# A fused Nyström attention and gated FFN kernel: Newton's S as 32 moving columns, and B's block forms made from PSUM

## Chip, cores, metric

One core of a Trainium2 chip. The metric is the device time of one execution in microseconds (us), taken by the device; medians and ranges are given over repeated executions. Slow runs of the kernel before are left out of its medians. Ratios are the mean time of one kernel's fast runs over the mean of the other's fast runs of the same rounds, so they are not quite the ratio of the medians that stand beside them. The intervals are 95% intervals.

## The reference, cut to what matters

```python
def _attn_ref(q, k, v):                      # q, k, v: 8 x 8 x 576 x 64
    m = 32
    q_lm = q.reshape(B, H, m, S // m, D).mean(axis=3)
    k_lm = k.reshape(B, H, m, S // m, D).mean(axis=3)
    A, Bm, C = sm(q, k_lm), sm(q_lm, k_lm), sm(q_lm, k)      # softmaxes
    Z = Bm^T / (|Bm|_1 * |Bm|_inf + 1e-06)
    for _ in range(6):
        Z = 2 * Z - Z @ Bm @ Z               # Newton's iteration, 32 x 32 for each head
    return A @ Z @ C @ v
# then, over the 4608 tokens: sigmoid(x @ w_gate) * (x @ w_val) @ w_out
```

The eight batches are woven together: while the tensor engine (PE) does the FFN of one batch, it also does the small attention matrices of the next.

The other engines bear their names of the profile: DVE is the vector engine, ACT the scalar engine, POOL is GpSimd, SP the SyncE, which issues DMAs, and PEld stands for the PE's weight loads. SBUF and PSUM are the two memories that the kernel puts its tiles in; it hands PSUM out in eight banks (BANKS = 8). Names of tiles that come up below: bs, sl and sa are the scores of B, C and A; cv is C·v; rtp turns the inverse row sums of A (rhl); an is A itself, made with them. `up` multiplies the rest of the attention (WT) into w_gate and w_val, which gives U and V; gp and vp are A times U and V, th the sigmoid's part of gp, ht the gated product, op the product with w_out, and ob its copy on the way out. s_5k and s_5q are the landmark sums of batch 5's k and q, from which GpSimd makes klm and bq.

## The kernel before

Four heads stand on the 128 partitions and two such groups lie side by side, so one 32 x 32 matrix for each of the eight heads is a tile of 128 x 2 x 32. To multiply it on the PE in one go it is spread into a **block form** of 128 x 128, with zeros off the blocks (`blk` is the mask of zeros and ones). Newton's iteration is kept as S = Z·B together with Y = Z·(C v): each step is S ← 2S − S·S and Y ← 2Y − S·Y. S is symmetric, so it serves as the fixed operand as it is.

```python
        # mid(b): B, its transpose, the square that Newton starts from
        E = sb.tile([128, 2, m], FP32, ...)
        act.activation(out=E, in_=bs, func=AF.Exp, scale=scale2)     # bs: PSUM
        ...                                                          # rs, rr: row sums on DVE
            act.mul(out=Bc[:, g, :], in_=E[:, g, :], mul=rr[:, g:g + 1])       # late batches
        dve.transpose(out=Bt..., in_=Bc...)
        spread(bdT, Bt)                                              # dve.tensor_mul with blk
        ...
            mm(out=s0[g], lhsT=bdT[:, g], rhs=bdT[:, g], ...)        # 128 columns
        s_at = [each(b, g).mul(sy[:, g, 0:128], s0[g], rc[:, g:g + 1]) ...]
        spread(bd, Bc)

        # newton(b), six iterations
                lo = 0 if it < ITERS - 1 else 128
                yield need(sy, banks=1)
                pn = bank([128, 2, 128 + D - lo], FP32, ...)
                for g in range(2):
                    mm(out=pn[:, g, :], lhsT=sy[:, g, 0:128], rhs=sy[:, g, lo:128 + D], ...)
                if lo == 0:
                    nsy = sb.tile([128, 2, 128 + D], BF16, ...)
                    dve.scalar_tensor_tensor(
                        out=nsy, in0=sy, scalar=2.0, in1=pn, op0=ALU.mult, op1=ALU.subtract)

        # front(b): the two halves of the landmark sums change places through DMA
                for c in range(2):
                    nc.sync.dma_start(out=other[what][64 * c:64 * c + 64], in_=s4[64 - 64 * c:128 - 64 * c])
```

The order of instructions is fixed when the kernel is built. A small model of the engines (the **recorder** below) is kept while the program is written down: it holds for every tile when it will have landed and for every engine when it will be free, and each time the PE has room it picks the next piece of work among those whose inputs have landed by then. `yield need(bd)` means "not before bd has landed".

The softmax here doesn't subtract the row's maximum and nothing guards it: scores larger than these inputs give would overflow.

## Time and profile before

| | before |
|---|---|
| median, range | 271.59 us, 271.58 to 271.88 (3 runs) |
| span of the profiled execution | 269.7 us |
| PE busy | 260.1 us, 96% |
| DVE busy | 193.3 us, 72% |

**Content** is the streaming time of all PE work in the built order (columns at 2.4 to the ns, but no less than 25 ns, plus 2 ns, plus 95 ns for each turn into or out of packed 32-column work; in the trace of before, matmuls of 512, 192, 96 and 32 columns start 216, 82, 42 and 25 ns behind their like, medians, and the 68 turns of the prediction have medians of 96 ns in and 95 out). **Waiting** is how much the start of a matmul in the trace falls behind the content ahead of it; I give how much it grows from 50 us on, where the kernel has its steady form. Before has 252.2 us of content and 4.0 us of waiting. These 4.0 are in part a residue of how I price the work: in the trace of e6 below, which has the same order and lacks no matmul, about 2 us of them stand at packed groups and the matmuls behind them, the rest in small pieces elsewhere. So only differences of waiting between kernels mean something.

### The profile page before, as it was taken

To read this page: it belongs to the slowest core of one execution; us is meant where nothing else is said; L and a number is where in the kernel's file an instruction comes from. 1 tells how busy PE (TensorE), PEld (TensorE's weight loads), DVE (VectorE), ACT (ScalarE), POOL (GpSimd) and SP (SyncE) were. 2 spreads that over 40 slices of the span, in tenths; PEclk is the share of its full clock that TensorE was granted. 3 is DMA by queue.
4 is the path that set the end of the run, shared out by engine and by line. 5 is a ranking of instruction groups with operands and counts; after the bars stand their busy time and mean duration, and the time that the engine had idled before them with its cause. 6 is when DMAs were issued, how large, how long until landed. Compare 5 with 4: busy or idle time off the path is not lost.

```text
span 269.7 us, 8019 instructions
## 1 busy us (share of the span) xinstructions
PE 260.1 (96%) x3089; PEld 167.0 (62%) x3123; DVE 193.3 (72%) x551; ACT 159.4 (59%) x413; POOL 96.2 (36%) x107
## 2 busy tenths in 40 slices
PE   8999999999999999999999999999999999999994
PEld 5877777757664666556646665556636664665443
DVE  4566888976899788948986778848968786963111
ACT  3663876866647754876477655875368643964001
POOL 8523231960874039511953078212922000000000
PEclk9999999999999999999999999999999999999999
DMA  6999999999795998889794989589530413101433
GB/s 94 193 206 205 205 206 206 205 203 172 141 194 115 204 170 121 181 135 199 141 221 72 182 157 203 129 139 199 124 90 12 97 41 80 41 0 41 117 103 92
DMA packets 62645, 38.00 MB, mean 141 GB/s; under 512 B 33552, under 2 KB 58128, under 8 KB 62608
## 3 DMA queue, kind: packets, MB, share of 16 engines
q0 software_dynamic: 23600, 18.88, 47.0%
q1 hardware_dynamic: 38896, 18.52, 31.4%
q8 instruction: 24, 0.39, 0.6%
q14 instruction: 13, 0.11, 0.1%
q10 hardware_dynamic: 112, 0.10, 0.1%
HBM read 37.75 MB, written 9.44 MB: 175 GB/s over the span
## 4 chain that ended last, share of the span: by engine, by line
PE 93%; ACT 2%; issue 2%; POOL 1%; DVE 0%; POOLq 0%; ACTq 0%
PE op L247 34%; PE gp L247 18%; PE vp L247 18%; PE idle_ps L247 3%; PE pn L247 2%; PE cv L247 2%; PE rb L247 2%; PE sc L247 1%; PE sa L247 1%; PE tp_q L252 1%; PE up_1g L247 1%; PE up_0g L247 1%; PE up_2g L247 1%; PE tp_k L252 1%; PE up_1v L247 1%
## 5 line engine op out<-in xcount | busy, mean ns | idle before, releaser
L247 PE MATMUL op<-wo_sb,ht 128*128 128x512 bf16 (+1 forms) x410 | 109.4, 373 | 2.1 <-issue 1.1
L153 ACT ACTIVATE th<-gp 128x288 bf16<-128x288 f32 x192 | 76.7, 415 | 48.4 <-PE gp L247 36.7
L153 DVE SCALAR_TENSOR_TENSOR ht<-th,vp 128x288 bf16<-128x288 bf16 x192 | 82.0, 448 | 21.9 <-ACT th L153 17.2
L247 PE MATMUL gp<-an,U 128*128 128x288 bf16 x384 | 78.5, 286 | 0.3
L247 PE MATMUL vp<-an,V 128*128 128x288 bf16 x384 | 78.4, 286 | 0.0
L247 PEld LDWEIGHTS <-ht 128*128 128x128 bf16 x444 | 39.9, 98 | 26.7 <-issue 5.8
L247 PEld LDWEIGHTS <-U 128*128 128x128 bf16 x384 | 35.9, 98 | 27.3 <-issue 2.5
L247 PEld LDWEIGHTS <-V 128*128 128x128 bf16 x384 | 37.5, 98 | 9.7 <-issue 0.2
L153 ACT ACTIVATE ob<-op 128x512 f32<-128x512 f32 (+1 forms) x31 | 18.2, 587 | 29.6 <-PE op L247 24.2
L153 DVE SCALAR_TENSOR_TENSOR sy<-sy,pn 128x384 bf16<-128x384 bf16 x35 | 19.2, 548 | 2.3 <-PE pn L247 1.9
L153 DVE TENSOR_SCALAR ob<-op 128x512 f32<-128x512 f32 (+2 forms) x7 | 4.2, 596 | 17.3 <-PE op L247 17.3
L247 PE MATMUL idle_ps<-idle_w 128*128 128x256 bf16 x86 | 14.8, 308 | 1.2 <-DVE idle_w L297 1.2
L247 PE MATMUL pn<-sy 128*128 128x192 bf16 (+1 forms) x84 | 13.1, 237 | 0.4 <-ACT kT L153 0.3
L153 DVE TENSOR_TENSOR an<-aexp,rb 128x384 bf16<-128x384 bf16 (+1 forms) x32 | 12.4, 446 | 0.3 <-PE rb L247 0.3
L247 PEld LDWEIGHTS <-sy 128*128 128x128 bf16 x88 | 8.1, 97 | 6.2 <-DVE sy L153 2.8
L153 ACT ACTIVATE aexp<-sa 128x288 bf16<-128x288 f32 x32 | 10.7, 418 | 1.5 <-PE sa L247 1.1
L247 PEld LDWEIGHTS <-idle_w 128*128 128x128 bf16 x86 | 8.5, 109 | 3.3 <-DVE idle_w L297 1.2
L247 PEld LDWEIGHTS <-WT 64*32 64x32 bf16 x384 | 3.8, 89 | 9.1 <-issue 6.6
L270 POOL DMA_DIRECT2D kn<-in_k_dram x9 | 7.0, 779 | 4.6 <-DMA wg_sb<-in_moe_w_gate_dram 2.1
L153 DVE CAST U<-up_0g 128x512 bf16<-128x512 f32 x8 | 5.5, 690 | 4.1 <-PE up_0g L247 4.1
L270 POOL DMA_DIRECT2D vn<-in_v_dram x8 | 6.3, 789 | 5.3 <-PE gp L247 4.5
L270 POOL DMA_DIRECT2D qn<-in_q_dram x9 | 6.8, 753 | 4.0 <-PE sm L247 2.2
(201 smaller groups left out, 349.7 us busy)
## 6 DMA issues: line engine op xcount, KB each, us to landing
vn<-in_v_dram POOLq DMA_DIRECT2D x8, 576.0 KB, 9.4
kn<-in_k_dram POOLq DMA_DIRECT2D x7, 576.0 KB, 8.1
qn<-in_q_dram POOLq DMA_DIRECT2D x7, 576.0 KB, 10.6
out_dram<-ob SPq DMA_DIRECT2D x53, 64.0 KB, 3.0
out_dram<-ob SPq DMA_DIRECT2D x17, 192.0 KB, 2.3
out_dram<-ob SPq DMA_DIRECT2D x18, 128.0 KB, 2.4
wg_sb<-in_moe_w_gate_dram POOLq DMA_DIRECT2D x3, 512.0 KB, 19.7
wv_sb<-in_moe_w_val_dram POOLq DMA_DIRECT2D x3, 512.0 KB, 21.0
```

Of the source, the lines that this page charges most:

```text
L153: f(**kw)
L247: nc.tensor.matmul(**kw)
L252: nc.tensor.transpose(**kw)
L270: nc.gpsimd.dma_start(out=t[:, hs], in_=src[b, hs].rearrange("h (p c) d -> p h (c d)", p=P6))
```

## The change

Its intent: in batches 2 to 7 the S part of the moving operand needs only 32 columns, because the product of a block form with a 32-column S is again a 32-column S. So `pn` shrinks from 192 to 96 columns. Since the fixed operand must still be the block form, the DVE has to make one (`sd`) in every step. Separately, B's block form `bd` is made straight from the exponentials in PSUM, B's transpose is made on the PE (`Bp`), and `bdT` is made from PSUM.

```diff
-        E = sb.tile([128, 2, m], FP32, name=f"E_{b}", tag="E")
+        late = b >= LATE
+        E = bs if late else sb.tile([128, 2, m], FP32, name=f"E_{b}", tag="E")
...
+        if late:
+            for g in range(2):
+                dve.scalar_tensor_tensor(
+                    out=bd[:, g], in0=E[:, g, None, :].to_broadcast([128, NP, m]),
+                    scalar=rr[:, g:g + 1], in1=blk, op0=ALU.mult, op1=ALU.mult)
+            yield need(bd, banks=1)
+            Bt = bank([128, 2, m], FP32, f"Bp_{b}")
+            for g in range(2):
+                mm(out=Bt[:, g], lhsT=bd[:, g], rhs=four, start=(g == 0), stop=(g == 1))
+        else:
+            (the DVE transpose, as before)
+        if b >= COMPACT:                                   # COMPACT = 2
+            Bs = sb.tile([128, 2, m], BF16, name=f"Bt_{b}", tag="Bt")
+            act.copy(out=Bs, in_=Bt)
...
-            mm(out=s0[g], lhsT=bdT[:, g], rhs=bdT[:, g], ...)
+            mm(out=s0[g], lhsT=bdT[:, g], rhs=Bs[:, g] if b >= COMPACT else bdT[:, g], ...)
...
-                    mm(out=pn[:, g, :], lhsT=sy[:, g, 0:128], rhs=sy[:, g, lo:128 + D],
+                    mm(out=pn[:, g, :], lhsT=sd[:, g], rhs=sy[:, g, lo:w + D],      # w = 32
...
+                    if compact:
+                        new = p[:, 2 * (w + D):].rearrange("p (g x) -> p g x", g=2)   # PSUM
+                        dve.scalar_tensor_tensor(
+                            out=new, in0=sy[:, :, 0:m], scalar=2.0, in1=pn[:, :, 0:m],
+                            op0=ALU.mult, op1=ALU.subtract)
                     nsy = ...                              # as before, 192 elements in place of 384
+                    if compact:
+                        sd = sb.tile([128, 2, NP, m], BF16, ...)
+                        dve.tensor_mul(
+                            out=sd, in0=blk[:, None].to_broadcast([128, 2, NP, m]),
+                            in1=new[:, :, None, :].to_broadcast([128, 2, NP, m]))
```

(cut: the constants, batch 0 and 1, the first `sd`, the norm's small tile moved to PSUM)

More of the change, by code (lines that the diff above doesn't have):

```diff
@@ L217 @@
     SWAP = 3
+    COMPACT = 2
     consts = ctx.enter_context(tc.tile_pool(name="consts", bufs=1))
@@ L350 @@
     model.free["dve"], model.free["act"] = 5.4, 6.6
+    four = consts.tile([128, m], BF16, name="four")
+    nc.vector.tensor_reduce(
+        out=four, in_=ident.rearrange("p (i l) -> p l i", i=NP), axis=AX.X, op=ALU.max)
     front_of, sums_of, lm_of, value_of, mid_of, norm_of, an_of, uv_of, step_at = ({} for _ in range(9))
-    square_of, turned_c, q_of = {}, {}, {}
+    square_of, turned_c, q_of, sd_of = {}, {}, {}, {}
     def copy(out, in_):
@@ L610, in mid @@
                 act.mul(out=Bc[:, g, :], in_=E[:, g, :], mul=rr[:, g:g + 1])
-        Bt = sb.tile([128, 2, m], BF16, name=f"Bt_{b}", tag="Bt")
-        dve.transpose(out=Bt.rearrange("p g l -> p (g l)"), in_=Bc.rearrange("p g l -> p (g l)"))
         bdT = sb.tile([128, 2, NP, m], BF16, name=f"bdT_{b}", tag="bdT")
         bd = sb.tile([128, 2, NP, m], BF16, name=f"bd_{b}", tag="bd", bufs=3)
+        if late:
[8 more added lines that the diff above has]
+        else:
+            Bt = sb.tile([128, 2, m], BF16, name=f"Bt_{b}", tag="Bt")
+            dve.transpose(out=Bt.rearrange("p g l -> p (g l)"), in_=Bc.rearrange("p g l -> p (g l)"))
+        if b >= COMPACT:
+            Bs = sb.tile([128, 2, m], BF16, name=f"Bt_{b}", tag="Bt")
+            act.copy(out=Bs, in_=Bt)
         def spread(dst, src):
+            if late:
+                return dve.tensor_mul(
+                    out=dst, in0=blk[:, None].to_broadcast([128, 2, NP, m]),
+                    in1=src[:, :, None, :].to_broadcast([128, 2, NP, m]))
             for g in range(2):
@@ L627, in mid @@
         yield need(model.landed[Bc.name] + (0.25 if b else 0.0), banks=1)
-        n1 = bank([128, 2, m], FP32, f"n1_{b}")
+        n1_cc = bank([128, 2 * m + 2], FP32, f"n1_{b}")
+        n1 = n1_cc[:, 0:2 * m].rearrange("p (g l) -> p g l", g=2)
         mm(out=n1, lhsT=blk, rhs=Bc, start=True, stop=(b > 0))
@@ L631, in mid @@
             mm(out=n1, lhsT=eps, rhs=idle_w[:, 0:2 * m], start=False, stop=True)
-        ce = sb.tile([128, 2], FP32, name=f"cc_{b}", tag="cc")
+        ce = n1_cc[:, 2 * m:] if b > 0 else sb.tile([128, 2], FP32, name=f"cc_{b}", tag="cc")
         dve.tensor_reduce(out=ce, in_=n1, axis=AX.X, op=ALU.max)
@@ L638, in mid @@
         dve.reciprocal(out=rc, in_=ce)
-        apart = 2 if b == 0 else 1
+        apart, w = 2 if b == 0 else 1, m if b >= COMPACT else 128
         yield need(bdT, banks=apart)
-        s0 = [bank([128, 2 // apart, 128], FP32, f"s0_{b}{x}") for x in range(apart)]
+        s0 = [bank([128, 2 // apart, w], FP32, f"s0_{b}{x}") for x in range(apart)]
         s0 = [s0[g % apart][:, g // apart] for g in range(2)]
         for g in range(2):
-            mm(out=s0[g], lhsT=bdT[:, g], rhs=bdT[:, g], start=(g == 0 or b == 0), stop=(g == 1 or b == 0))
-        sy = sb.tile([128, 2, 128 + D], BF16, name=f"sy_{b}_0", tag="sy0", bufs=2)
+            mm(out=s0[g], lhsT=bdT[:, g], rhs=Bs[:, g] if b >= COMPACT else bdT[:, g],
+               start=(g == 0 or b == 0), stop=(g == 1 or b == 0))
+        sy = sb.tile([128, 2, w + D], BF16, name=f"sy_{b}_0", tag="sy0", bufs=2)
         if b == 0:
             model.by_part.add(sy.name)
-        s_at = [each(b, g).mul(sy[:, g, 0:128], s0[g], rc[:, g:g + 1]) for g in range(2)]
+        s_at = [each(b, g).mul(sy[:, g, 0:w], s0[g], rc[:, g:g + 1]) for g in range(2)]
         if b == 0:
             square_of[b] = [(sy, s_at)]
-        spread(bd, Bc)
+        elif b >= COMPACT:
+            sd_of[b] = sb.tile([128, 2, NP, m], BF16, name=f"sd_{b}_0", tag="sd", bufs=2)
+            for g in range(2):
+                dve.scalar_tensor_tensor(
+                    out=sd_of[b][:, g], in0=s0[g][:, None, :].to_broadcast([128, NP, m]),
+                    scalar=rc[:, g:g + 1], in1=blk, op0=ALU.mult, op1=ALU.mult)
+        if not late:
+            spread(bd, Bc)
         aexp = sb.tile([128, 2, S], BF16, name=f"aexp_{b}", tag="aexp", bufs=2)
@@ L667, in scale_y @@
                 dve.tensor_mul(out=ysc, in0=rcs, in1=rc)
-                y_at = [each(b, g).mul(sy[:, g, 128:128 + D], cv[g], ysc[:, g:g + 1])
+                y_at = [each(b, g).mul(sy[:, g, w:w + D], cv[g], ysc[:, g:g + 1])
                         for g in range(2)]
@@ L671, in scale_y @@
                 y_at = [dve.tensor_scalar(
-                    out=sy[:, g, 128:128 + D], in0=cv[g], scalar1=rcs[:, g:g + 1],
+                    out=sy[:, g, w:w + D], in0=cv[g], scalar1=rcs[:, g:g + 1],
                     scalar2=rc[:, g:g + 1], op0=ALU.mult, op1=ALU.mult) for g in range(2)]
@@ L802, in newton @@
             sy, bd, _ = mid_of[b]
+            compact = b >= COMPACT
+            w = m if compact else 128
+            sd = sd_of.pop(b) if compact else sy[:, :, 0:128]
             y6 = sb.tile([128, 2, 2, D], BF16, name=f"y6_{b}", tag="y6")
             for it in range(ITERS):
-                lo = 0 if it < ITERS - 1 else 128
-                yield need(sy, banks=1)
-                pn = bank([128, 2, 128 + D - lo], FP32, f"pn_{b}_{it}")
+                last = it == ITERS - 1
+                lo = w if last else 0
+                yield need(sy, *((sd,) if compact else ()), banks=1)
+                p = bank([128, 2 * (w + D - lo) + 2 * m * (compact and not last)], FP32, f"pn_{b}_{it}")
+                pn = p[:, 0:2 * (w + D - lo)].rearrange("p (g x) -> p g x", g=2)
                 for g in range(2):
-                    mm(out=pn[:, g, :], lhsT=sy[:, g, 0:128], rhs=sy[:, g, lo:128 + D],
+                    mm(out=pn[:, g, :], lhsT=sd[:, g], rhs=sy[:, g, lo:w + D],
                        start=(g == 0), stop=(g == 1))
-                if lo == 0:
-                    nsy = sb.tile([128, 2, 128 + D], BF16, name=f"sy_{b}_{it + 1}", tag="sy", bufs=3)
+                if not last:
+                    if compact:
+                        new = p[:, 2 * (w + D):].rearrange("p (g x) -> p g x", g=2)
+                        dve.scalar_tensor_tensor(
+                            out=new, in0=sy[:, :, 0:m], scalar=2.0, in1=pn[:, :, 0:m],
+                            op0=ALU.mult, op1=ALU.subtract)
+                    nsy = sb.tile([128, 2, w + D], BF16, name=f"sy_{b}_{it + 1}", tag="sy", bufs=3)
                     dve.scalar_tensor_tensor(
                         out=nsy, in0=sy, scalar=2.0, in1=pn, op0=ALU.mult, op1=ALU.subtract)
+                    if compact:
+                        sd = sb.tile([128, 2, NP, m], BF16, name=f"sd_{b}_{it + 1}", tag="sd", bufs=2)
+                        dve.tensor_mul(
+                            out=sd, in0=blk[:, None].to_broadcast([128, 2, NP, m]),
+                            in1=new[:, :, None, :].to_broadcast([128, 2, NP, m]))
+                    else:
+                        sd = nsy[:, :, 0:128]
                     sy = nsy
@@ L820, in newton @@
                             out=y6[:, g],
-                            in0=sy[:, g, None, 128:128 + D].to_broadcast([128, 2, D]), scalar=2.0,
+                            in0=sy[:, g, None, w:w + D].to_broadcast([128, 2, D]), scalar=2.0,
                             in1=pn[:, g, None, :].to_broadcast([128, 2, D]),
```

## The prediction

> **What bounds the kernel now.** I read the page's engine line first, then the chain that ended last, the stretches by engine, and the timeline of PE and DVE around one batch's Newton iteration.
>
> ```profile
> PE 260.1 (96%) x3089; PEld 167.0 (62%) x3123; DVE 193.3 (72%) x551; ACT 159.4 (59%) x413; POOL 96.2 (36%) x107
> PE   8999999999999999999999999999999999999994
> PE 93%; ACT 2%; issue 2%; POOL 1%; DVE 0%; POOLq 0%; ACTq 0%
> ...
> L247 PE MATMUL pn<-sy 128*128 128x192 bf16 (+1 forms) x84 | 13.1, 237 | 0.4 <-ACT kT L153 0.3
> ```
>
> The PE is busy 96% of the span, every slice but the first and last is at 9, and 93% of the chain is PE; DVE has no share of it. So time is the sum of what the PE streams, and a cut of PE columns is worth its own length as long as other PE work stands where it was. The 237 ns of a pn matmul is its latency; what it costs the PE is the distance to the next start.
>
> ```profile
> 97.92 0.33 PE L247 MATMUL pn<-sy 128*128 128x192 bf16 x2
> 98.08 0.41 PE L247 MATMUL sm<-blk,aexp 128*128 128x4 bf16 x10
> ...
> 99.27 0.33 PE L247 MATMUL pn<-sy 128*128 128x192 bf16 x2
> 99.43 0.59 PE L247 MATMUL op<-wo_sb,ht 128*128 128x512 bf16 x2
> ```
>
> A pair of 192-column pn matmuls takes 0.16 us of the PE (97.92 to 98.08, 99.27 to 99.43), 80 ns each.
>
> DVE is the second engine. In the steady stretches its busy time is 23 to 24 us in 30:
>
> ```profile
> 121.00:151.00 30.00, 29.63 (x331) 18.28 (x334) 23.24 (x66) 19.74 (x55) 13.81 (x14) 1.00 0.94 162
> 211.00:241.00 30.00, 29.53 (x311) 18.58 (x315) 24.34 (x66) 18.06 (x45) 0.00 (x0) 1.00 0.24 58
> ```
>
> (columns: length, then PE, PEld, DVE, ACT, POOL busy with their counts). And inside a Newton iteration it is nearly full, other work standing between the sy steps:
>
> ```profile
> 130.75 0.55 DVE L153 SCALAR_TENSOR_TENSOR sy<-sy,pn 128x384 bf16<-128x384 bf16 x1
> 131.22 1.54 DVE L153 TENSOR_TENSOR an<-aexp,rb 128x384 bf16<-128x384 bf16 x4
> 132.68 0.55 DVE L153 SCALAR_TENSOR_TENSOR sy<-sy,pn 128x384 bf16<-128x384 bf16 x1
> 133.14 0.81 DVE L153 SCALAR_TENSOR_TENSOR ht<-th,vp 128x288 bf16<-128x288 bf16 x2
> 133.87 0.54 DVE L153 SCALAR_TENSOR_TENSOR sy<-sy,pn 128x384 bf16<-128x384 bf16 x1
> ```
>
> A step of 0.55 us holds the DVE 0.47 (130.75 to 131.22): instructions with no wait between them overlap by about 0.08.
>
> [...] 192 columns take 80 ns; the 96-column tp_q transposes take 0.52 us for 12 in the chain, 43 ns each; the 32-column lm_0q matmuls 0.67 for 24, 28 ns each[...]. [...] an takes 546 ns at 384 elements and 346 at 192, 1.04 ns per element. [...] the waiting pair cc (starts 93.35) and ce (93.60) stands 0.25 apart though cc takes 0.22, without the overlap. [...] the order of the changed kernel has bdT wait for the ACT copy that reads the same Bp.
>
> **The change part by part.** (a) *Newton, batches 2 to 7.* Five of six iterations, two matmuls each: 60 matmuls go from 192 to 96 columns, 80 ns to 43. 60 x 37 = 2.2 us of PE removed. The last iteration keeps its 64 columns. (b) *The square s.* Per batch two of 128 columns (0.11 us a pair by start times) become two of 32 (0.056): 6 x 0.054 = 0.3 removed. (c) *B transposed on the PE.* Twelve Bp matmuls of 32 columns: 12 x 28 ns = 0.3 added, cancelling (b). Counting all columns in the two built orders gives the same: 2.4 us fewer, or 2.2 with the small matmuls' fixed costs.
>
> (d) *Moves.* The built order shows what the diff does not. The PE enters or leaves the packed 32-column work (up, bs, sl, sa, cv) 94 times in place of 88: sa and cv of a batch stood side by side and no longer do. From the starts in the trace, each such turn costs 95 ns beyond the columns (68 turns after 50 us, median 96 in and 95 out). 6 x 0.095 = 0.57 us added. The idle filler matmuls (86) and everything on the PE up to batch 2 are in the same order.
>
> (e) *DVE.* Before, a Newton step holds it 0.47 us. After, it is three: a 64-element write of the new S into PSUM, the 192-element sy, which waits for it, and the 256-element block form sd. My estimates from rows above: 0.25 (as cc, 64 elements with a waiting follower), 0.27 (346 less 0.08), and 346 + 64 x 1.04 - 80 = 0.33; together 0.85. That is 0.38 more, 30 times: 11.4 us. The one-offs of a batch go from about 1.36 us (transpose, bdT, sy scaling, bd) to 1.7 (bd from PSUM 0.53, bdT 0.33, sy 0.33, sd 0.53): 2 us over six. Four WT copies move to ACT (-1.4), five ob evacuations come from ACT (+3). DVE busy should be about 208 us, 77%, and the chain from pn to the next weights grows from 0.55 to about 0.93.
>
> Does it stay beside the PE? In batch 5, from pn_0 to wtp, the changed order gives the PE 10.8 us of streaming (8.6 before). DVE has there 5 x 0.85 + four an 1.46 + two y 0.40 + nine ht x 0.365 = 9.4 us. Before it had about 8.75 against 8.6. So the scheduler has put more work into the gaps: the shortest gap between two pn pairs is 1.3 us (it was 0.9), against 0.2 for the result to reach DVE plus 0.93. The slack is about 0.15 us at the tightest, so I allow 0.2 us of PE waiting in the whole kernel.
>
> The longer Newton delays U and V. After the last gp of batches 1 to 6 the PE runs 26, 20, 32, 34, 40, 26 op matmuls before the next batch's first gp, where it ran 10, 0, 0, 12, 22, 32. This costs nothing while finished rows are left: 88 op matmuls still stand after the last vp (104 before), and the tail stays dense op.
>
> Sum: -2.2 - 0.3 + 0.3 + 0.57 + 0.2 = -1.4, and 271.59 - 1.4 = 270.2. The larger column count (-2.4) would give 270.0. I say **270.1 us**.
>
> **Rivals.** *DVE becomes the bound.* For it: 14 us more on an engine at nine tenths in many slices, and the three dependent steps take the place of one. Its mark would be PE idle before sd weight loads. If half of the 30 iterations stalled 0.1 us the loss is 1.5 us and the time 271.5; if each lost the whole 0.38 us it would be 11 us and 281. Against it: PE work in the gaps has been raised with it, and DVE waits 17.2 us for th and 17.3 for the last op, so it has room. I put the real stall under 1 us. *The gain stands whole and the moves cost nothing.* For it: the six extra turns may stand next to gaps that existed anyway, or some of the DVE waits of the weight loads (sy 2.8 us in eleven times after 56 us) may go away with longer gaps. Then 269.1. *The saving goes into waiting at a batch's end:* U and V come later, ffn1 starts later, and the finished rows run out. It would add microseconds in batches 5 to 7. The 88 op matmuls left (19 us) speak against it.
>
> **Range and chances.** The PE terms of (a) to (c) are sure to 0.2 us; the turns to 0.3 either way; the stalls from 0 to 1. The best case is 269.0, the plausible bad case 271.2; I give 269.0 to 271.2. Two per cent is 5.4 us. More than twice the removed columns would be needed to get faster by that, and slower by that needs a stall of nearly 0.3 us in every iteration. So 0.01 faster, 0.97 within, 0.02 slower.
>
> **What would show each step.** Right: pn<-sy,sd pairs 0.085 us apart; PE busy down by about 2 us in the steady stretches while its idle stays; sd, sy and new rows of about 413, 346 and 210 ns with new and sy not overlapping; DVE busy near 208; no wait of PEld for sd over 2 us in all; the last 20 us dense op. Wrong: PEld waiting on DVE sd for several us (the DVE rival), PE idle after a batch's last gp (the third rival), or rows of the PSUM-to-PSUM step far from 210 ns. A drop to 269 or under would mean the turns were free.

## More of the kernel before

The recorder's times are estimates, but the order that comes out of them is what the chip runs. Where the recorder is wrong, the PE stands.

The engine line, the PE's row and the chain are in the prediction. They show a kernel without one long wait: the PE is busy everywhere and has 93% of the chain that ends last. What remains of a change to such a kernel has to be read from two sums: what the PE streams, and what it waits.

## The result

| | before | after |
|---|---|---|
| median, range | 271.63 us, 271.58 to 271.88 (4 runs) | 274.57 us, 274.11 to 276.34 (4 runs) |
| ratio | | 1.0118 [1.0073, 1.0163] |
| span of the profiled execution | 269.7 | 272.3 |
| content / waiting after 50 us | 252.2 / 4.0 | 250.3 / 8.7 |
| turns into or out of packed work | 88 | 94 |

Within 2%, as said, but 4.5 us above the number and outside the range: not a gain of 1.4 us but a loss of 2.9. The content fell by 1.9 us, the waiting rose by 4.7, and −1.9 + 4.7 = 2.8 is the loss, within 0.2 us (the profiled spans differ by 2.6).

The page of the kernel after, its engine line, its chain and the row of the new pn:

```profile
PE 263.4 (97%) x3135; PEld 165.8 (61%) x3135; DVE 205.1 (75%) x612; ACT 159.7 (59%) x419; POOL 96.0 (35%) x107
...
PE 85%; DVE 4%; ACT 4%; DMA 3%; issue 2%; POOL 1%; DVEq 0%; ACTq 0%; POOLq 0%
...
L249 PE MATMUL pn<-sy,sd 128*128 128x96 bf16 (+1 forms) x72 | 8.8, 205 | 0.0
```

PE "busy" rose by 3.3 us though less is streamed. That row misleads here: the trace before lacks 34 matmul records (3,089 against 3,123 weight loads, 3,135 of both after), and the length of a matmul is not what it takes of the PE (a pn of 96 columns lasts 206 ns, and the second of a pair starts 43 ns after the first; medians of the kernel after). The chain is the better witness: DVE, ACT, DMA and POOL now have 12% of it, where ACT and POOL had 3% and DVE none.

In the two stretches that the prediction shows, DVE is busy 24.55 and 25.50 us of 30, 1.2 to 1.3 more than before, and PE 29.49 and 29.59 (before 29.63 and 29.53). The rows of one step, from the view of the tile pn:

```profile
L153 DVE SCALAR_TENSOR_TENSOR pn<-sy,pn x30: 218/222/229, 75.6 to 232.9; 128x64 f32<-128x64 bf16 x30
L153 DVE TENSOR_TENSOR sd<-blk,pn x30: 414/414/416, 76.1 to 233.5; 128x256 bf16<-128x256 bf16 x30
```

(shortest, median and longest in ns). 222 and 414 ns were estimated as 210 and 413. So the operations cost what they should. What the PE waits for is elsewhere. The waits of PE and its weight loads after 50 us (in total, times, longest), before:

```profile
PEld L247 <- DVE sy L153: 2.8, 11, 0.4
PEld L247 <- POOL bq L153: 0.3, 1, 0.3
```

and after:

```profile
PEld L249 <- DVE sd L153: 2.0, 9, 0.3
PEld L249 <- DVE bd L153: 1.9, 4, 1.0
PEld L249 <- POOL bq L153: 1.1, 2, 0.7
PE Bp L249 <- DVE bd L153: 0.8, 2, 0.5
```

The wait that the DVE rival named, PEld for sd, is smaller than the wait for sy was. The new ones are **bd** and **bq**.

**bd.** Batch 2 in the timeline of DVE, ACT and PE of the kernel after, in order of time (start, length; in brackets the idle time ahead and what ended it):

```profile
65.21 0.17 DVE L153 RECIPROCAL rr<-rs 128x2 f32<-128x2 f32 x1
65.77 0.45 ACT L153 ACTIVATE Bc<-bs,rr 128x32 bf16<-128x32 f32 x2
66.26 0.61 DVE L153 SCALAR_TENSOR_TENSOR bd<-bs,rr,blk 128x128 bf16<-128x128 f32 x2 [0.88 <-ACT Bc L153]
66.67 0.45 PE L249 MATMUL Bp<-four,bd 128*128 128x32 bf16 x2 [0.50 <-DVE bd L153]
```

bd needs rr, which is there at 65.38. It starts at 66.26, when the ACT's Bc has ended. Bc and bd need nothing of each other; both read the exponentials in the bank of bs. The built program makes bd wait for Bc all the same: DVE is idle for 0.88 us and is released by Bc, while in e3 below, where the exponentials stand in SBUF, bd starts 0.04 us behind rr. I call this wait for the other reader of the bank the exclusion. In the whole kernel DVE idles 3.5 us so, six times (0.53 us in batch 5). The recorder keeps banks apart when they are taken and freed, but does not know of this exclusion: it lets bd start when rr has landed, and puts Bp in the order by that. The PE comes to Bp too early and stands.

**bq.** Batch 5, the queue of the SyncE in the kernel after, then in the kernel before:

```profile
128.94 7.91 SPq L1008 DMA_DIRECT2D out_dram<-ob  x4
136.95 1.14 SPq L485 DMA_DIRECT2D s_5k<-s_5k  x2
141.86 0.79 SPq L1008 DMA_DIRECT2D out_dram<-ob  x2
142.75 1.11 SPq L485 DMA_DIRECT2D s_5q<-s_5q  x2
```

```profile
133.34 1.16 SPq L480 DMA_DIRECT2D s_5k<-s_5k  x2
138.25 1.12 SPq L480 DMA_DIRECT2D s_5q<-s_5q  x2
```

GpSimd has s_5k ready at 133.77 and s_5q at 138.66 in the kernel after (the ends of its rows at 132.25 and 137.16). They leave 3.2 and 4.1 us later, behind stores of output that stand ahead of them in the same queue and are not yet ready. Before, s_5q was ready at 138.22 and left at 138.25. Then GpSimd's bq comes late and the PE stands:

```profile
144.79 1.52 POOL L153 TENSOR_TENSOR bq<-s_5q 64x256 bf16<-64x256 f32 x2 [2.95 <-DVE U L153]
```

```profile
146.37 0.31 PE L249 MATMUL sl<-kT,bq 64*32 64x288 bf16 x7 [0.45 <-POOL bq L153]
```

The bracket of the POOL row names DVE's U, which ends at 144.63; by its DMA record the first half of s_5q lands at the same 144.63, and it is this half that bq reads.

By place, the growth of the waiting in the kernel after is about 2.9 us at Bp and the matmuls next to it (the vp of batches 4 and 7 among them, 0.5 us each), 1.0 us at bq in batch 5, and some 1.2 us in steps of 0.2 us at rtp, sa and one pn.

### The profile page after: what moved, and what is told of

Same layout as the page of the kernel before. It is cut to its first block, busy times and chain, and to the rows that moved or that the text cites.

```text
span 272.3 us, 8172 instructions
## 1 busy us (share of the span) xinstructions
PE 263.4 (97%) x3135; PEld 165.8 (61%) x3135; DVE 205.1 (75%) x612; ACT 159.7 (59%) x419; POOL 96.0 (35%) x107
## 4 chain that ended last, share of the span: by engine, by line
PE 85%; DVE 4%; ACT 4%; DMA 3%; issue 2%; POOL 1%; DVEq 0%; ACTq 0%; POOLq 0%
PE op L249 33%; PE vp L249 16%; PE gp L249 16%; DMA qn<-in_q_dram 3%; PE idle_ps L249 2%; PE pn L249 2%; PE rb L249 2%; ACT aexp L153 1%; PE sa L249 1%; PE sc L249 1%; PE tp_q L254 1%; PE up_0g L249 1%; PE cv L249 1%; PE up_1g L249 1%; DVE U L153 1%
## 5 line engine op out<-in xcount | busy, mean ns | idle before, releaser
L249 PE MATMUL op<-wo_sb,ht 128*128 128x512 bf16 (+1 forms) x444 | 110.9, 374 | 0.0
L153 DVE SCALAR_TENSOR_TENSOR ht<-th,vp 128x288 bf16<-128x288 bf16 x192 | 80.3, 449 | 11.0 <-ACT th L153 8.9
L249 PEld LDWEIGHTS <-ht 128*128 128x128 bf16 x444 | 38.8, 98 | 30.3 <-issue 5.0
L153 ACT ACTIVATE ob<-op 128x512 f32<-128x512 f32 (+2 forms) x27 | 15.7, 581 | 28.3 <-PE op L249 21.9
L153 DVE TENSOR_SCALAR ob<-op 128x512 f32<-128x512 f32 (+1 forms) x11 | 7.2, 655 | 16.1 <-PE op L249 16.0
L153 DVE SCALAR_TENSOR_TENSOR sy<-sy,pn 128x192 bf16<-128x192 bf16 (+1 forms) x35 | 13.3, 381 | 1.7 <-PE pn L249 0.7
L153 DVE TENSOR_TENSOR sd<-blk,pn 128x256 bf16<-128x256 bf16 x30 | 12.4, 414 | 0.0
L249 PEld LDWEIGHTS <-sd 128*128 128x128 bf16 x72 | 6.5, 97 | 7.7 <-DVE sd L153 2.0
L249 PE MATMUL pn<-sy,sd 128*128 128x96 bf16 (+1 forms) x72 | 8.8, 205 | 0.0
```

The lines of the kernel that those rows point to most:

```text
L153: f(**kw)
L249: nc.tensor.matmul(**kw)
```

## The experiments

Theory A: B's part costs waits because bd is placed ahead of the exclusion with Bc. Theory B: Newton's saving is real, and eaten by waits that the longer DVE step makes. Theory C: the swaps stand in the SyncE's queue. The rival to all: the saving of content was never there, or some operation is slower than its row says.

| run | content | turns | waiting after 50 us | median us | before, fast runs of the same chip | ratio |
|---|---|---|---|---|---|---|
| before | 252.2 | 88 | 4.0 | | | 1 |
| after | 250.3 | 94 | 8.7 | 274.57 | 271.63 | 1.0118 [1.0073, 1.0163] |
| e1 Newton only | 250.0 | 94 | 7.4 | 272.82 | 272.94 | 1.0008 [0.9977, 1.0038] |
| e2 B only | 252.7 | 90 | 6.9 | 275.02 | 272.94 | 1.0098 [1.0060, 1.0136] |
| e3 E in SBUF | 250.3 | 94 | 7.3 | 273.39 | 272.94 | 1.0034 [0.9990, 1.0078] |
| e4 order knows | 249.9 | 90 | 6.6 | 272.26 | 272.94 | 0.9993 [0.9952, 1.0034] |
| e5 after, swaps by GpSimd | 250.3 | 94 | 9.1 | 274.90 | 271.73 | 1.0132 [1.0083, 1.0181] |
| e6 before, swaps by GpSimd | 252.2 | 88 | 4.0 | 272.03 | 271.73 | 0.9991 [0.9960, 1.0022] |
| e7 e1 with swaps by GpSimd | 250.0 | 94 | 6.0 | 271.91 | 271.73 | 0.9999 [0.9968, 1.0030] |
| e8 e4 with swaps by GpSimd and more | 250.3 | 94 | 8.1 | 274.16 | 271.73 | 1.0071 [1.0031, 1.0112] |
| e9 e4, sd from the S in SBUF | 250.5 | 96 | 11.6 | 277.45 | 271.82 | 1.0195 [1.0169, 1.0222] |
| e10 e7, sd from the S in SBUF | 249.8 | 92 | 16.2 | 281.09 | 271.82 | 1.0334 [1.0300, 1.0368] |
| e11 before, one more DVE op a step | 252.3 | 90 | 7.5 | 274.40 | 271.82 | 1.0080 [1.0051, 1.0110] |
| e12 e2, order knows | 252.7 | 90 | 4.4 | 272.42 | 271.82 | 1.0015 [0.9990, 1.0040] |
| e13 e9, mask in PSUM, 7 banks | 251.4 | 100 | 11.8 | 281.16 | 271.72 | 1.0342 [1.0319, 1.0365] |
| e15 e4, 7 banks | 251.4 | 100 | 11.9 | 282.07 | 271.72 | 1.0362 [1.0334, 1.0391] |

All give a correct result. The waiting is that of one profiled execution. In the round of e1 to e4 the fast runs of before were themselves spread from 271.48 to 273.34 (two slow ones, of 275.93, are left out), so the intervals are wide.

**e1_newton_only**: Newton's part without B's.

```diff
-        late = b >= LATE
+        late = False
...
-            Bs = sb.tile([128, 2, m], BF16, name=f"Bt_{b}", tag="Bt")
-            act.copy(out=Bs, in_=Bt)
+            Bs = Bt
```

> Newton's S as 32 columns alone; B and its block forms as before (E in SBUF, DVE transpose, bd and bdT from SBUF, no Bp). Theory B-path (the loss is the stalls around Bp and bd, where in the changed kernel Bp waited 0.9 us in batch 2 and 0.7 in batch 5 and vp stood 0.5 us in batches 4 and 7): the compact Newton is a gain by itself; PE content from the built order is 250.0 us against 252.2 before, so 269.5 to 270.5. Theory Newton (12 us more DVE work makes DVE late everywhere): it is as slow as the whole change, 273.5 to 275.

Same time as before within a wide interval; the profiled span is 1.2 us longer (270.9 against 269.7). Its content is 2.2 us lower: less for pn and s, more for six turns. Against it stand 3.4 us of waiting. Of the waiting, bq in batch 6 has 1.15 us in the same way as bq in batch 5 above; the rest comes in pieces of 0.15 to 0.3 us.

**e2_b_only**: B's part without Newton's.

```diff
-    COMPACT = 2
+    COMPACT = 99
```

> B's block forms from PSUM alone; Newton with 128 columns as before. PE content 252.7 us against 252.2. Theory B-path: slower than before by its stalls, 274 to 276, with PE waiting for bd at Bp. Theory Newton: within 1 us of before, 271.5 to 272.6.

This part alone costs about 1%, nearly all that the whole change loses. Its content is 0.5 us over before, its waiting 2.9 us over, and the waits name it:

```profile
PEld L249 <- DVE bd L153: 3.2, 8, 1.0
PE Bp L249 <- DVE bd L153: 0.8, 2, 0.5
```

**e3_e_sbuf**: the whole change, but the exponentials in SBUF, so that bd and Bc share no bank. The PE's order is the same as in the kernel after.

```diff
-        E = bs if late else sb.tile([128, 2, m], FP32, name=f"E_{b}", tag="E")
+        E = sb.tile([128, 2, m], FP32, name=f"E_{b}", tag="E")
```

> The whole change, but E is written to SBUF and not back into its PSUM bank: the instruction order is the same on every engine; bd and Bc no longer read one PSUM bank, so bd need not wait for Bc, and the bank comes free at once. Theory bank (bd waits for the ACT reads of the same bank, which the recorded schedule does not know): DVE's idle before bd (3.5 us in six) and PE's waits for bd (1.9 us) go, 271 to 272.5. If the stalls have another cause: 274 to 275 as the change.

```profile
65.19 0.61 DVE L153 SCALAR_TENSOR_TENSOR bd<-E,rr,blk 128x128 bf16<-128x128 f32 x2
```

```profile
PEld L249 <- DVE bd L153: 0.2, 1, 0.2
PEld L249 <- POOL bq L153: 1.7, 2, 1.1
```

With the shared bank gone and the order unchanged, bd of batch 2 starts at once behind rr (which ends at 65.15), and the wait for bd falls from 1.9 to 0.2 us; the 0.8 of Bp's own wait is gone. That is the direct proof of theory A. The stall at bq in batch 5 stays and is a little longer, so the waiting as a whole falls only by 1.4 us, from 8.7 to 7.3. The ratio falls from 1.0118 to 1.0034, though the two intervals still overlap a little.

**e4_order_knows**: the whole change, the bank shared, but the recorder is told that bd cannot start before Bc has landed.

```diff
+            model.waits[bd.name] = model.landed[Bc.name]
             for g in range(2):
                 dve.scalar_tensor_tensor(out=bd[:, g], ...
```

> The whole change with the same instructions; only the recorded order is made with bd starting no earlier than Bc ends. PE content 249.9 us (90 turns in place of 94). Theory order (the stalls come from Bp being placed too early): Bp no longer waits, 271 to 272.5. Theory that the exclusion itself or DVE load costs the time: 274 or more.

The ratio falls from 1.0118 to 0.9993: one line in the recorder takes the whole loss away, though not to a gain. Waits for bd are gone; 6.6 us of waiting remain against 4.0. The line changes the order in many other places too, and e8 below shows that another order alone can move the time; e3, where the order stays, is free of this doubt.

**e5_swap_pool, e6_before_swap_pool, e7_newton_swap_pool**: the swaps issued by GpSimd and not by the SyncE, in the kernel after, in before (a control) and in e1. The PE's order stays that of the kernel it comes from.

```diff
-                    nc.sync.dma_start(out=other[what][...], in_=s4[...])
+                    nc.gpsimd.dma_start(out=other[what][...], in_=s4[...])
```

> The whole change, with the four small copies per batch that swap landmark halves (s to s, batches 3 to 7) started by the GpSimd queue and not by SP's. The order of PE instructions is the same. Theory queue: in the changed kernel these copies stood behind output stores that waited for their ob tile (s_5k was ready at 133.8 and left SP at 137.0, s_5q ready at 138.7 and left at 142.8), bq came late, and PE lost 1.0 us at bs and sl of batch 5. Then PE's waits for POOL bq go and the time falls by about 1 us, ratio to before about 1.008 where the change has 1.012. If the queue doesn't matter: no change beyond 0.3 us.

> Control: the kernel before with the same move of the copies. It had 0.3 us of waits for POOL bq. Theory queue: within 0.4 us of before. More than 0.5 us faster would mean that the move helps by itself and e5 must be read against this.

> The compact Newton alone with the same move. Newton alone lost 1.15 us at bs and sl of batch 6 for a late POOL bq. Theory queue: 1.1 us less than Newton alone, so ratio to before about 0.996 to 0.997, the first version faster than before. Theory Newton (DVE work): still 1.0 or above, with PE waiting on sd (4.2 us of waits of the weight loads, of which little is lost PE time).

The control is unchanged. In e7 the stall at bq is gone and waiting falls from 7.4 to 6.0; so theory C holds there, for 1.4 us of waiting, of which the ratio to before shows only 0.0009, far less than its interval. In e5 the stall of batch 5 is gone too, but one of the same size stands in batch 7 (0.60 and 0.72 us from 206.7 on), and the time is no better: a miss for theory C in the whole change.

**e8_order_swap_pool**: e4 with the swaps by GpSimd, with bdT told to wait for the copy Bs, and with DVE steps with a scalar column charged 0.06 us more in the recorder (in the kernel after, sd<-s,rc,blk takes 343 ns with a column, and y<-sy,pn, of 128 elements too, 281 without).

```diff
-            columns = sum(k in aps for k in ("scalar1", "scalar2", "mul"))
+            columns = sum(k in aps for k in ("scalar1", "scalar2", "mul", "scalar"))
...
+            model.waits[bdT.name] = model.landed[Bs.name] if late else 0.0
```

> The whole change, the copies moved, and the recorded order made with bd after Bc, bdT after the ACT copy that reads the same bank, and 0.06 us for the per-partition scalar of the fused DVE operations. PE content 250.3 us. Theory order plus queue: PE waits for bd and for bq both gone, 0.5 to 1.5 us faster than before (ratio 0.995 to 0.998). If the loss is DVE load itself: no faster than before.

A miss: 1.0071, worse than e4. Three edits at once give another order (94 turns where e4 has 90, 0.4 us more content, 1.5 us more waiting). I did not take them apart, so which of them it is stays open.

**e12_b_order_knows**: e2 with the line of e4.

> B's part alone (as e2) with the recorder told that bd cannot start before the ACT copy Bc has landed. PE work 252.7 us as e2's. Theory (e2's loss is the Bp matmuls placed 0.6 us too early because the shared bank's exclusion was not in the recorded schedule): weight loads wait for bd under 0.5 us (e2: 3.2), waiting after 50 us falls from 6.9 to 4.3 to 5.0 us, ratio 1.002 to 1.004 where e2 had 1.0098. Rival (two engines reading one bank slow each other, or B's chain is too long for the order): waits move elsewhere and the ratio stays at 1.007 or above.

Waiting falls from 6.9 to 4.4 us and the ratio from 1.0098 to 1.0015. No wait for bd is left, though DVE idles ahead of bd as it did in the kernel after: in the first of these lines, from the timeline of DVE in batch 2, it is still 0.88 us; the others, from the PE's, show that the PE now has other work until bd is there (at 66.78), and Bp starts with no wait at all.

```profile
66.17 0.61 DVE L153 SCALAR_TENSOR_TENSOR bd<-bs,rr,blk 128x128 bf16<-128x128 f32 x2 [0.88 <-ACT Bc L153]
```

```profile
66.41 0.59 PE L249 MATMUL op<-wo_sb,ht 128*128 128x512 bf16 x2
66.84 0.20 PE L249 MATMUL Bp<-four,bd 128*128 128x32 bf16 x2
```

So theory A is shown from both sides: the exclusion taken away under a fixed order (e3), and the order taught under a fixed exclusion (e4, e12). In e4 and e12 the exclusion as such costs the PE no wait that the trace shows; not knowing of it does.

**e11_before_longer_step**: theory B from the other side. The kernel before, with one more DVE operation in each of 30 Newton steps, whose result nobody reads.

```diff
+                    if more:                               # batches 2 to 7, not the last step
+                        dve.scalar_tensor_tensor(
+                            out=p[:, 384:512]..., in0=sy[:, :, 0:64], scalar=2.0, in1=pn[:, :, 0:64],
+                            op0=ALU.mult, op1=ALU.subtract)
                     dve.scalar_tensor_tensor(out=nsy, in0=sy, scalar=2.0, in1=pn, ...)
```

(cut: pn's tile p made 128 elements longer)

> The kernel before, with one more DVE operation in each of the first five Newton steps of batches 2 to 7, ahead of sy and waited for by it: 128 elements written to PSUM that nobody reads, some 0.3 us on DVE and on the chain, counted by the recorder as the change's own steps are. PE work is that of before (252.3 us, 90 turns against 88). Theory (a longer DVE step by itself makes the PE wait, about 2 us for 0.38 us a step): waiting after 50 us rises from 4.0 to 5.3 to 6 us, ratio 1.005 to 1.009. Rival (DVE has room, the waits of the change come from something else in it): waiting 4.0 to 4.6 and ratio 0.999 to 1.003.

```profile
L153 DVE SCALAR_TENSOR_TENSOR pn<-sy,pn x30: 282/289/296, 76.2 to 227.3; 128x128 f32<-128x128 bf16 x30
```

```profile
PEld L247 <- DVE sy L153: 4.5, 14, 0.5
```

0.29 us more on the DVE's chain, thirty times, with the PE's content unchanged, go with a loss of 0.8%; the wait for sy grows from 2.8 to 4.5 us. The waiting, 7.5 us, is above the 5.3 to 6 expected: about 1.4 us of it stand at 72 us, ahead of the first added operation, behind a DVE step of two elements that took 1.56 us where it takes 0.17 in before. That row (ce<-cc, from 68.30 to 69.86) starts just after a GpSimd operation (68.20 to 69.84) and ends just after it. It looks like the rows of e9, below, though ce has a single tensor operand, and is not the theory; without it 6.1 us are left against 4.0. Whether the other executions have this meeting too is not shown; if they do, about half of the 0.8% is its, and not the step's. The profiled execution was also the slowest of six (275.23 us, the others 273.69 to 274.94). So with a longer DVE step the PE waits about 2 us more, the same size as what Newton's part gives back in e7. The recorder counts the added operation, so the order is not quite that of before either.

**e9_sd_from_sy, e10_newton_sd_from_sy**: take time away from the step. The block form is made from the bf16 S that the step has written to SBUF, and the write of the new S to PSUM goes.

```diff
-                    if compact:
-                        new = ...
-                        dve.scalar_tensor_tensor(out=new, ...)
...
-                            in1=new[:, :, None, :].to_broadcast([128, 2, NP, m]))
+                            in1=nsy[:, :, None, 0:m].to_broadcast([128, 2, NP, m]))
```

> The whole change with the order taught (as e4), and the separate write of the new S into PSUM taken out: the block form is made from the bf16 S that the step has just written to SBUF (the same numbers). Before to after of one DVE step: 222 + 354 + 414 ns of rows become about 354 + 300, so 30 times 0.3 us, some 8 us, of DVE work are gone, and the chain from pn to the next weights is about 0.25 us shorter. The built order has 250.5 us of streamed PE work with 96 turns (e4 249.9 with 90; before 252.2 with 88). Theory (the longer DVE step is what gave Newton's 2 us back): the PE's waiting after 50 us falls from e4's 6.6 us to 5 to 5.5, DVE busy from some 205 to some 197, ratio to before 0.993 to 0.998. Rival (the waits come from the order and the buffers, whatever the step's length): waiting stays at 6 to 7 and the ratio is 1.000 to 1.003, above e4's by the six turns.

> Newton's part alone with the swaps queued by GpSimd (as e7), with the block form made from the bf16 S in SBUF: no write of the new S to PSUM, a DVE step 0.3 us shorter. Built order: 249.8 us of PE work, 92 turns (e7: 250.0, 94; before 252.2). Theory (the longer step costs the waits): waiting after 50 us falls from e7's 6.0 us to 4.3 to 5.0, weight loads wait for sd well under e7's 4.0 us, and the ratio to before is 0.993 to 0.996: the first version faster than before by what its interval can show. Rival: waiting stays near 6, ratio 0.998 to 1.001 as e7.

The largest misses: 2.0% and 3.3% slower than before. The sd rows tell why, from the view of the tile sd in e9, then in e10 (shortest, median, longest):

```profile
L153 DVE TENSOR_TENSOR sd<-blk,sy x30: 291/300/1250, 76.0 to 235.5; 128x256 bf16<-128x256 bf16 x30
```

```profile
L153 DVE TENSOR_TENSOR sd<-blk,sy x30: 291/556/1755, 76.3 to 240.3; 128x256 bf16<-128x256 bf16 x30
```

The longest in e10, in the timelines of GpSimd (POOL), DVE and PE:

```profile
106.17 1.64 POOL L153 TENSOR_TENSOR s_4q<-qT 128x768 f32<-128x768 bf16 x1
```

```profile
106.21 1.75 DVE L153 TENSOR_TENSOR sd<-blk,sy 128x256 bf16<-128x256 bf16 x1
```

```profile
108.02 0.26 PE L249 MATMUL pn<-sy,sd 128*128 128x96 bf16 x2 [1.32 <-DVE sd L153]
```

By itself the operation takes 291 ns here, less than the 414 it takes from PSUM in the kernel after. When it starts just after a GpSimd operation it ends just after that one ends (107.81 and 107.96). All five of batch 7, where GpSimd has nothing left to do, take 291 to 293 ns. Each of the rows above 500 ns overlaps a GpSimd operation that began before it and ends about 0.15 us after that one's end. What the 30 rows take beyond 291 ns adds up to 5.7 us in e9 and 11.9 in e10, where the waiting is 5.0 and 10.2 us above that of e4 and e7. In the kernel after, where sd is made from PSUM, 17 of its 30 rows begin while a GpSimd TENSOR_TENSOR runs, and all 30 take 414 to 416 ns. So the write of the new S to PSUM, which looks like a detour of 222 ns, is what keeps Newton's step clear of GpSimd. In the kernel before one such meeting is visible, a bd<-blk,Bc of 860 ns where the median is 216: of the sixteen it is the only one that begins beside a GpSimd TENSOR_TENSOR (69.13 to 69.99, GpSimd's s_3k from 68.27 to 69.91). In the trace of the kernel after no DVE row is stretched so (bd from PSUM takes 342 to 352 ns); but none of its twelve bd from PSUM begins beside GpSimd, so that B's block forms gain from PSUM in the same way is not shown.

**e13_mask_in_psum, e15_order_knows_7**: the same cut of the step without the meeting. The mask is kept in PSUM, so that sd has one operand in SBUF. The mask takes a bank; e15 is e4 with as many banks.

```diff
-    BANKS = 8
+    BANKS = 7                              # e13 and e15
...
+    blk_ps = ps.tile([128, NP, m], FP32, name="blk_ps", tag="blk", bufs=1)      # e13 alone
...
-                            out=sd, in0=blk[:, None].to_broadcast([128, 2, NP, m]),
+                            out=sd, in0=blk_ps[:, None].to_broadcast([128, 2, NP, m]),
```

> As e9 (whole change, order taught, block form made from the bf16 S without the write of the new S to PSUM), but the mask that the block form is multiplied with is kept in PSUM, so that the operation has only one operand in SBUF. The mask holds one of the eight banks, so seven are left for everything else; e15 is the same count of banks without the shorter step. Built orders of both: 251.4 us of PE work, 100 turns. Theory on e9 and e10 (their sd steps were stretched because both operands lay in SBUF while GpSimd worked): every sd row lies near 350 to 420 ns, no row over 500. Theory on the step's length: waits 1 to 2.5 us fewer than e15, time 1 to 2.5 us less than e15. Rival (the step's length does not matter): within 0.5 us of e15. Against before it loses to the bank: ratio 1.01 to 1.02.

> e4 with seven PSUM banks in rotation in place of eight, everything else alike: the base that e13 is to be compared with. The order has 251.4 us of PE work (e4: 249.9) and 100 turns (90), and fewer banks to hide waits behind: 4 to 7 us over e4, ratio to before 1.015 to 1.025. If banks are not short, the ratio stays under 1.008.

In e13, from the view of the tile sd:

```profile
L153 DVE TENSOR_TENSOR sd<-blk_ps,sy x30: 423/424/426, 77.9 to 243.9; 128x256 bf16<-128x256 f32 x30
```

With one operand in PSUM no row is stretched: the reading of e9 and e10 holds. The waits for sd, e15 and then e13:

```profile
PEld L249 <- DVE sd L153: 5.4, 19, 0.5
```

```profile
PEld L249 <- DVE sd L153: 2.2, 6, 0.5
```

They fall by 3.2 us, but the time only by 0.9 (281.16 against 282.07, with overlapping intervals), and the waiting as a whole is the same: small waits elsewhere (for th 1.1 us against 0.5, for rt 0.5 against none) come in their place. The two orders have the same content and turns, but they are not the same order. So with seven banks the length of the step sets where the PE waits, and hardly how long. Seven banks in place of eight cost e4 3.7% (1.0362 against 0.9993), about 10 us where 4 to 7 were expected: this kernel has no bank to spare. Whether a shorter step would bring the 2 us back with all eight banks is not shown.

## Why the prediction was wrong

*PE columns (a, b, c) and turns (d)*: right. The term was −2.2 − 0.3 + 0.3 + 0.57 = −1.6 us, and the built orders, priced with figures of the trace, have −1.9. The kernel without B's part (e1) has 6 turns more and 2.2 us less content, where −2.2 − 0.3 + 0.57 = −1.9 follows from the prediction. The trace after has the pn pairs and rows as named.

*DVE (e)*: the sizes were right, the consequence was not. Rows of 222, 354 and 414 ns against 210, 346 and 413; DVE busy 205.1 against 208. The comparison of sums in a batch (9.4 us of DVE beside 10.8 of PE) said too little: such sums can show that DVE is no bound, not that each result comes in time. And part of the room that the prediction read was not where the steps are: of the 17.3 us that DVE waits for op, 16.7 stand after 246 us in the trace before, and the last Newton step there is over by 226. Nor is a stall of "nearly 0.3 us in every iteration" needed for 2%: the 7 us from 270.1 to 277 are 0.23 us in each of 30.

*The failed step*: "so I allow 0.2 us of PE waiting in the whole kernel", and with it the range, which let "the stalls" go from 0 to 1. They measured 4.7 us. The range was tight by the prediction's own account too: its mild case of the DVE rival, 271.5, lay above the upper end of 271.2. What stood in its place:

1. B's part, about 2.5 us (e2's 6.9 us of waiting against e12's 4.4): bd waits for Bc because both read one bank (0.88 us in batch 2; none in e3, where they do not), and the recorded order did not know it. I had seen a wait of the same kind at bdT, named it in the prediction, and not asked it of bd, the operand that the change moved to a shared bank. That is the largest part of the miss, and e3, e2 and e12 settle its cause.
2. Newton's part, about 2 us (e7's 6.0 against 4.0): waits of 0.15 to 0.3 us spread over the batches. In e11 a longer DVE step by itself goes with as much. The prediction counted 30 steps with 0.15 us of slack as free; it named the rival, with the mark "PE idle before sd weight loads", and that mark did not come in the kernel after (2.0 us for sd, 2.8 for sy before). It did in e1 and e7, where it was 4.2 and 4.0 us. By place, e7's 2.0 us over e6 are about 0.5 at pn itself, 0.6 at s (which waits for bdT), 0.5 at packed groups and what follows them, and small pieces elsewhere. So the rival is likely right in substance, but that the longer step makes all of the 2 us is argued and not shown. e9 and e10, meant to show it, failed for another reason, and in e13 a shorter step moved the waits only.
3. The swaps in the SyncE's queue, about 1 us in the kernel after. The prediction did not look at this queue. That the stall goes when the queue is changed is shown (e7); that it would shorten the whole change is not (e5).

The three overlap and add to more than 4.7.

*The third rival* (waiting at a batch's end for finished rows) did not come: in the page's row of the PE every slice but the first two and the last is at 9.

No version beat the kernel before by more than its interval. The best of the change is e4 at 0.9993.

## What to carry to other kernels

Where a tuned order is recorded ahead of the run, price a change twice: the work it removes, and every dependency it adds that the recorder does not model; the operand that was moved to a PSUM bank here brought along waits for the other engine that reads that bank (DVE idle for 3.5 us in six places). A saving spread over many small pieces, each in front of a chain that grows by a few tenths of a microsecond, is easily turned into as many small waits; the test is to lengthen the chain in the old kernel and see what that costs. And before removing an operation that looks like a detour through PSUM, ask which engine it keeps out of the way of (here the same block form took 414 to 416 ns from PSUM, and 291 to 1,755 from SBUF beside GpSimd).
